# Channel products of an fp32-accurate token mixer: seven block products in place of eight

## The chip, the cores and the metric

One Trainium2 chip, one core of it. The metric is the device time of one execution in microseconds (us), the median of several runs. The engines are TensorE (PE, matmuls; PEld is its weight load), VectorE (DVE), ScalarE (ACT), GpSimd (POOL) and SyncE (SP, which issues the transfers).

## The reference, cut to what matters

An RWKV attention (8 heads of 48, 768 steps, batch 2) feeds a gated MLP with a token mix, and its result x (2, 768, 384) feeds the mixer that the change is about:

```python
def _moe2_ref(x, w_tok1, w_tok2, w_ch1, w_ch2) -> np.ndarray:
    xt = x.transpose(0, 2, 1)
    h = np.maximum(xt @ w_tok1, 0.0) @ w_tok2       # 768 -> 256 -> 768, over tokens
    u = x + h.transpose(0, 2, 1)
    h2 = np.maximum(u @ w_ch1, 0.0) @ w_ch2         # 384 -> 1536 -> 384, over channels
    return (u + h2).astype(np.float32)
```

The two products of the second line of h2 run over 2 x 768 = 1536 tokens. Everything is float32.

## The kernel before, in words

Each float32 operand is kept as two tiles, a rounded high part and the low rest, and `prod` (L254) makes one product as three matmuls into one PSUM tile: high times high (L257), high weight times low data (L258), low weight times high data (L259). The high part is written by ScalarE, the low part by a subtraction on VectorE or GpSimd. The weights arrive as 64-bit words and are converted in three stages (`advance`: two ScalarE instructions L214 and L215, two VectorE instructions L217 and L219, then ScalarE L224 for the high and GpSimd or VectorE L226 for the low part).

The program is written out by hand: `ORDER` and `LAST` are strings of letters, and each letter emits one piece of work, so they set in which order every engine meets its instructions. `LAST` covers the gated MLP's end, the conversions of the last weights (digits 0, 1, 2), the token products T1 (`i`, `j`) and T2 (`k`, `l`), and, as letter `m`, the first channel product C1 of the first token group. Then `rest` (L483) emits what is left in loops.

The channels are handled transposed: channels on the 128 partitions, tokens along the columns. Tokens stand in four groups of 384. `C1(h, j)` makes 128 of the 1536 hidden channels for group h: 3 blocks of input channels by 3 matmuls of 384 columns, then `relu_split` (L396) writes the high part `ch` on ScalarE (L398) and the low part `cl` on VectorE (L399). `C2(h, j, ct)` adds that hidden block into output block ct: 3 matmuls of 384 columns into a PSUM tile that stays for all 12 values of j. `rest` emits C1 for group h+1 and C2 for group h in turn, so that a hidden block is ready long before it is used. At j = 11 VectorE adds the residual (L454) and SyncE stores 128 x 384 values (L455).

Early in the program, `outputs` (L612) adds an already made tile `av` into the PSUM tile `py` with an identity matmul (L617) for the first seven 128-token blocks, between groups of sixteen or more 48-row matmuls (L608 before it, L623 behind it), and `kv` (L635) does the same for a 112 x 112 state tile.

## Time and profile before

| what | value |
|---|---|
| median of 3 runs (lowest, highest) | 391.27 us (390.36, 391.82) |
| the profiled execution: its time, its span | 391.98 us, 390.3 us |
| TensorE's granted clock | 1.00 in each stretch from 0 to 385 us |
| TensorE busy | 379.9 us, 97 % of the span |
| VectorE, ScalarE, GpSimd busy | 233.5, 187.8, 133.1 us |
| 254 to 385 us: TensorE, VectorE, GpSimd busy | 130.57, 36.93, 4.95 us of 131 |

The span is the profiled execution alone; its time has 1.7 us more around it. Busy time of an engine that is not the bound may grow without cost as long as nothing waits for it. The attention and the first parts of the gated MLP run to about 150 us, the gated MLP's token mix and output to about 213 us, T1, T2 and the first C1 tiles to about 254 us, and `rest` from there to the end.

### The profile page before, as it was taken

To read this page: it belongs to the slowest core of one execution; us is meant where nothing else is said; L and a number is where in the kernel's file an instruction comes from. 1 tells how busy PE (TensorE), PEld (TensorE's weight loads), DVE (VectorE), ACT (ScalarE), POOL (GpSimd) and SP (SyncE) were. 2 spreads that over 40 slices of the span, in tenths; PEclk is the share of its full clock that TensorE was granted. 3 is DMA by queue.
4 is the path that set the end of the run, shared out by engine and by line. 5 is a ranking of instruction groups with operands and counts; after the bars stand their busy time and mean duration, and the time that the engine had idled before them with its cause. 6 is when DMAs were issued, how large, how long until landed. Compare 5 with 4: busy or idle time off the path is not lost.

```text
span 390.3 us, 7950 instructions
## 1 busy us (share of the span) xinstructions
PE 379.9 (97%) x3229; PEld 354.8 (91%) x3229; DVE 233.5 (60%) x396; ACT 187.8 (48%) x427; POOL 133.1 (34%) x149
## 2 busy tenths in 40 slices
PE   8899999999999999999999999999999999999994
PEld 3487788889999799999999999999999999999993
DVE  7999998889797575794486674782133114211320
ACT  3699878887345795754546674741111111111000
POOL 2325577763543356567544651350000000000000
PEclk9999999999999999999999999999999999999998
DMA  7575375453361014322433242400010001000110
GB/s 238 172 215 181 100 246 155 122 156 114 94 214 42 2 40 123 107 66 71 123 102 102 81 126 78 121 3 0 3 44 18 1 0 62 0 2 0 64 40 27
DMA packets 15581, 33.68 MB, mean 86 GB/s; under 512 B 2352, under 2 KB 5680, under 8 KB 15536
## 3 DMA queue, kind: packets, MB, share of 16 engines
q1 hardware_dynamic: 15536, 33.09, 27.9%
q8 instruction: 27, 0.44, 0.5%
q14 instruction: 18, 0.15, 0.1%
HBM read 30.72 MB, written 2.36 MB: 85 GB/s over the span
## 4 chain that ended last, share of the span: by engine, by line
PE 83%; POOL 4%; ACT 3%; issue 3%; DVE 3%; DMA 2%; SPq 1%; POOLq 0%; ACTq 0%
PE mm L257 23%; PE mm L258 23%; PE mm L259 23%; PE py L623 3%; PE pa L582 2%; PE py L608 2%; DMA st<-in_dram 1%; PE tr L282 1%; POOL vs L367 1%; PE pkv L641 1%; DMA kr<-in_dram 1%; PE mm L567 1%; PE mm L420 1%; PE py L617 1%; PE pt L595 1%
## 5 line engine op out<-in xcount | busy, mean ns | idle before, releaser
L399 DVE SCALAR_TENSOR_TENSOR cl<-mm,ch 128x384 fp32r<-128x384 f32 x48 | 26.5, 556 | 83.9 <-ACT ch L398 83.9
L398 ACT ACTIVATE ch<-mm 128x384 fp32r<-128x384 f32 x48 | 23.4, 492 | 93.1 <-PE mm L259 93.0
L217 DVE SCALAR_TENSOR_TENSOR st<-st 128x384 int32<-128x384 int32 (+1 forms) x50 | 30.3, 607 | 9.5 <-ACT st L215 7.9
L219 DVE SCALAR_TENSOR_TENSOR st<-st 128x384 int32<-128x384 int32 (+1 forms) x50 | 33.2, 665 | 1.7
L214 ACT ACTIVATE st<-st 128x384 f32<-128x384 f32 (+1 forms) x50 | 25.8, 517 | 9.3 <-DMA st<-in_dram 9.3
L588 POOL TENSOR_SCALAR_AFFINE_SELECT A<-A 128x512 f32<-128x512 f32 x24 | 18.3, 770 | 33.5 <-ACT A L587 32.0
L215 ACT ACTIVATE st<-st 128x384 int32<-128x384 uint32 (+1 forms) x50 | 25.5, 510 | 0.0
L369 ACT ACTIVATE gh<-vs 128x384 fp32r<-128x384 f32 x16 | 8.4, 524 | 32.9 <-POOL vs L367 32.9
L367 POOL TENSOR_TENSOR vs<-vs,uT 128x384 f32<-128x384 f32 x16 | 19.2, 1205 | 11.6 <-DVE vs L365 11.6
L560 POOL TENSOR_TENSOR rk<-kr 112x512 f32<-112x512 f32 x12 | 19.0, 1580 | 11.4 <-DMA kr<-in_dram 11.4
L257 PE MATMUL mm<-xt,wuh 128*128 128x256 f32 x72 | 20.8, 289 | 0.0
L259 PE MATMUL mm<-xt,wul 128*128 128x256 f32 x72 | 20.3, 282 | 0.0
L258 PE MATMUL mm<-xt,wuh 128*128 128x256 f32 x72 | 20.3, 282 | 0.0
L534 DVE TENSOR_TENSOR_SCAN wf<-wf,scan 112x516 f32<-112x516 f32 x12 | 19.0, 1583 | 1.6 <-DMA wf<-in_dram 1.6
L548 DVE TENSOR_TENSOR_SCAN wf<-wf,scan 112x516 f32<-112x516 f32 x12 | 17.8, 1480 | 0.4
L391 POOL TENSOR_TENSOR x1l<-x,x1h 128x384 fp32r<-128x384 f32 x12 | 14.0, 1173 | 10.4 <-ACT x1h L390 10.4
L125 PE MATMUL mm<-scan 112*128 112x512 bf16 x49 | 14.2, 431 | 3.1 <-DVE scan L673 1.7
L556 DVE TENSOR_TENSOR kr<-kr,wf 112x1024 f32<-112x1024 f32 x12 | 15.9, 1328 | 1.2 <-DVE wf L548 0.2
L257 PE MATMUL mm<-ch,c20h 128*128 128x384 f32 x48 | 16.1, 336 | 0.2 <-DVE o L454 0.2
L257 PE MATMUL mm<-woh,gh 128*128 128x384 f32 x48 | 16.2, 338 | 0.0
L259 PE MATMUL mm<-woh,gl 128*128 128x384 f32 x48 | 16.1, 336 | 0.0
L257 PE MATMUL mm<-uh,c10h 128*128 128x384 f32 x48 | 16.1, 336 | 0.0
(188 smaller groups left out, 1233.3 us busy)
## 6 DMA issues: line engine op xcount, KB each, us to landing
st<-in_dram SPq DMA_DIRECT2D x38, 384.0 KB, 3.4
kr<-in_dram SPq DMA_DIRECT2D x12, 448.0 KB, 4.3
st<-in_dram SPq DMA_DIRECT2D x18, 256.0 KB, 4.2
wf<-in_dram SPq DMA_DIRECT2D x12, 227.5 KB, 2.9
vn<-in_dram SPq DMA_DIRECT2D x12, 192.0 KB, 4.5
out_dram<-o SPq DMA_DIRECT2D x12, 192.0 KB, 1.9
bsg<-in_dram SPq DMA_DIRECT2D x2, 192.0 KB, 3.9
ub<-in_dram SPq DMA_DIRECT2D x1, 3.5 KB, 4.6
```

The source lines that it names most:

```text
L214: nc.scalar.activation(high.bitcast(F32), high.bitcast(F32), AF.Copy, scale=REBIAS)
L215: nc.scalar.activation(low, low.bitcast(U32), AF.Copy, scale=TOP3, bias=FLOOR)
L217: nc.vector.scalar_tensor_tensor(low, high, -2 ** 31, low, op0=ALU.bitwise_and, op1=ALU.bitwise_or)
L219: nc.vector.scalar_tensor_tensor(low, high, 3, low, op0=ALU.logical_shift_left, op1=ALU.bitwise_or)
L257: mm(out, w[0], x[0], start=first, stop=False, skip_group_check=True)
L258: mm(out, w[0], x[1], start=False, stop=False, skip_group_check=True)
L259: mm(out, w[1], x[0], start=False, stop=last, skip_group_check=True)
L367: nc.gpsimd.tensor_tensor(t, t, self.uT[d, h], op=ALU.mult)
L398: nc.scalar.activation(hi, ps, AF.Relu)
L399: nc.vector.scalar_tensor_tensor(lo, ps, 0.0, hi.bitcast(F32), op0=ALU.max, op1=ALU.subtract)
L534: nc.vector.tensor_tensor_scan(WF[i][:, WCOL + 2:], WF[i][:, :NHP * CW], scan1.rearrange("p h c -> p (h c)"), 0.0, op0=ALU.mult, op1=ALU.add)
L560: nc.gpsimd.tensor_tensor(RK[i][:PR], KR[i][:, 0], KR[i][:, 1], op=ALU.mult)
```

## The change

**Blocks.** Tokens stand in three groups of 512 columns, split in two halves of 256 (`ONE`, `TWO`). The T2 tiles, which were four of 384, are 512, 256, 256 and 512 wide (`EDGES`). The hidden channels go in 6 steps of 256 for each group, 18 steps in all.

**Seven for eight.** With weights cut in 2 x 2 blocks of 128 x 128 and tokens in two halves, a product of 2 x 2 blocks takes eight block products; Strassen's scheme in Winograd's form takes seven, of sums of blocks. `C2` does so for output blocks 0 and 1 in all 18 steps (digits `1` to `7`); output block 2 stays plain (`C2d`, digits `8`, `9`). The first channel product does so for groups 1 and 2 (`C1s`, letters `g` to `m`, seven products of 256 columns and two plain ones of 512 for the third input block); group 0 stays plain, with 512 columns (`C1`, letters `a`, `b`).

**Sums.** The left sums are made once: of the second weights on GpSimd (`A`, `B`), of the first weights on VectorE with the low parts on GpSimd (`C`, `D`). The sums of u for groups 1 and 2 are made on VectorE (`E`, `F`). In each step the results of `C1s` are added from PSUM into SBUF on VectorE, made positive and rounded on ScalarE (`o`, `q`), and VectorE makes two low parts (`p`, `r`), four sums of halves (`s`) and two low parts of these sums (`t`, `u`).

**Banks.** Five PSUM banks hold the four sums and output block 2 for all six steps of a group; three rotate for the first channel product. At a group's end `G` to `P`, `Q`, `S` put the sums together and store eighteen pieces of 128 x 256. The residual (`R`) is added on GpSimd.

**Order.** A new string `REST` sets the order of all this. The letter `m` leaves `LAST` and the rest of `LAST` closes up, with the conversions of the channel weights at earlier places. The identity matmuls of the early stage are split in two: 64 and 64 output rows for `py`, 64 and 48 for the state.

```diff
+G = 2 * P
+ONE, TWO = slice(0, G), slice(G, 2 * G)
+EDGES = 0, 4, 6, 8, 12
...
+REST = (
+    "abAzAc deBacB fAb12d efBaC3 587695 7EbaFc D412d6 38Fe94 c1Ab2d fBa38c 579CRe AD64b1 Bad23f 89cebg 57612d fhAijC "
...
-    def C1(self, h, j):
-        ps = self.mm(E)
-        c = slice(j * P, (j + 1) * P)
-        for k in range(3):
-            self.prod(ps, self.wp(f"c1{k}", 0, c, DCH), self.u[h, k], k == 0, k == 2)
-        hi, lo = self.a2(F32R, E, "ch"), self.a15(F32R, "cl")
-        self.relu_split(ps, hi, lo)
-        self.hid[h, j] = hi, lo
-
-    def C2(self, h, j, ct):
-        n = DCH // P
-        if j == 0:
-            self.cps[ct] = self.mm(E, self.ps3)
-            hi, lo = self.u[h, ct]
-            self.o[ct] = self.a15(nm="o")
-            self.nc.vector.tensor_tensor(self.o[ct], hi.bitcast(F32), lo.bitcast(F32), op=ALU.add)
-        c = slice(ct * P, (ct + 1) * P)
-        self.prod(self.cps[ct], self.wp(f"c2{j // 4}", j % 4, c, E), self.hid[h, j], j == 0, j == n - 1)
-        if j == n - 1:
-            nc = self.nc
-            o = self.o[ct]
-            nc.vector.tensor_tensor(o, self.cps[ct], o, op=ALU.add)
-            nc.sync.dma_start(self.out[ct * P:(ct + 1) * P, h * E:(h + 1) * E], o)
...
+    def left_sums(self, e, f):
+
+        t = self.st("sw")
+        a11, a21, a12, a22 = (f[:, q * P:(q + 1) * P] for q in range(4))
+        s1, s2, s3, s4 = (t[:, q * P:(q + 1) * P] for q in range(4))
+        e(s1, a21, a22, op=ALU.add)
+        e(s2, s1, a11, op=ALU.subtract)
+        e(s3, a21, a11, op=ALU.subtract)
+        e(s4, a12, s2, op=ALU.subtract)
+        return t
...
+    def split_sums(self, e, t, to, place):
+
+        for (hi, lo), x in ((to, t[:, :3 * P]), (place, t[:, 3 * P:])):
+            self.nc.scalar.activation(hi, x, AF.Copy)
+
+    def sums_of_c2(self, k):
+
+        if k == 0:
+            self.sum_tiles("s2")
+        i, b = k // 2, k % 2 * 2
+        hi, lo = (t.rearrange("p (k c) -> p k c", c=E)[:, b:b + 2, :2 * P].bitcast(F32) for t in self.w[f"c2{i}"])
+        f = self.st("f")
+        e = self.nc.gpsimd.tensor_tensor
+        e(f.rearrange("p (k c) -> p k c", k=2), hi, lo, op=ALU.add)
+        self.sw["s2", k] = self.left_sums(e, f)
...
+        e = self.nc.vector.tensor_tensor
+        for q in range(2):
+            hi, lo = (t.bitcast(F32) for t in self.wp(f"c1{q}", 0, slice(k * G, (k + 1) * G), DCH))
+            e(f[:, q * G:(q + 1) * G], hi, lo, op=ALU.add)
+        self.sw["s1", k] = self.left_sums(e, f)
...
+        for q in range(2):
+            hi, lo = self.u[n + 1, q]
+            f.append(self.st("f"))
+            e(f[q], hi.bitcast(F32), lo.bitcast(F32), op=ALU.add)
+        ta, tb = self.ut = [self.st("ta"), self.st("tb")]
+        e(ta[:, ONE], f[0][:, TWO], f[0][:, ONE], op=ALU.subtract)
+        e(ta[:, TWO], f[0][:, TWO], f[1][:, TWO], op=ALU.subtract)
+        e(tb[:, ONE], f[1][:, TWO], ta[:, ONE], op=ALU.subtract)
+        e(tb[:, TWO], f[1][:, ONE], tb[:, ONE], op=ALU.subtract)
...
+    def C1(self, n, b):
+
+        p = self.mm(2 * G)
+        for q in range(3):
+            self.prod(p, self.C1w(n, b, q), self.u[0, q], q == 0, q == 2)
...
+    def sub(self, o, x, y):
+        self.nc.vector.scalar_tensor_tensor(o, x, 0.0, y, op0=ALU.max, op1=ALU.subtract)
+
+    def C1a(self, n):
+        r, ta, tb, p = self.raw[n][:4]
+        self.sub(ta[:, ONE], p[:, TWO], r[:, ONE])
+        h, l = self.hid[n][0]
+        self.sub(l, p, h.bitcast(F32))
+
+    def C1b(self, n):
+        r, ta, tb, p1, p2 = self.raw[n]
+        self.sub(ta[:, TWO], p1[:, TWO], r[:, TWO])
+        self.nc.vector.tensor_tensor(tb[:, ONE], r[:, TWO], ta[:, ONE], op=ALU.subtract)
+        self.sub(tb[:, TWO], p2[:, ONE], tb[:, ONE])
+        h, l = self.hid[n][1]
+        self.sub(l, p2, h.bitcast(F32))
+        self.raw[n] = [ta, tb]
...
+    def right_split(self, n, j):
+        t = self.raw[n][j]
+        hi, lo = self.big("th", "t"), self.big("tl", "t")
+        self.nc.scalar.activation(hi, t, AF.Copy)
+        self.nc.vector.tensor_tensor(lo, t, hi.bitcast(F32), op=ALU.subtract)
+        self.hid[n].append((hi, lo))
...
+    def C1s(self, n, m):
+
+        g, k = divmod(n, DCH // G)
+        w = lambda q: self.C1w(k, 1, 0) if q == 3 else [t[:, q * P:(q + 1) * P] for t in self.ws["s1"][k]]
+        half = lambda v, c: [t[:, c] for t in v]
+        b, c, d, ta, tb = (self.u[g, q] for q in range(5))
+        p, act = self.prod, self.nc.scalar.activation
+        add = lambda o, i, j: self.nc.vector.tensor_tensor(o, i, j, op=ALU.add)
+        if m == 0:
+            self.raw[n] = [self.mm(2 * G) for _ in range(3)] + [self.temp(q) for q in ("sz", "p1", "p2")]
+        x, y, z, sz, c1, c2 = self.raw[n]
+        if m == 0:
+            p(z[:, ONE], self.C1w(k, 0, 0), half(b, ONE), True, True)
+            p(z[:, TWO], w(0), half(ta, ONE), False, True)
+            act(sz, z, AF.Copy)
+        elif m == 1:
+            p(x, self.C1w(k, 0, 2), d, True, False)
+            p(x[:, ONE], self.C1w(k, 0, 1), half(c, ONE), False, True)
+        elif m == 2:
+            p(x[:, TWO], w(3), half(c, TWO), False, True)
+            add(c1, x, sz)
+        elif m == 3:
+            p(z[:, ONE], w(1), half(tb, ONE), False, True)
+            add(c1[:, TWO], z[:, ONE], c1[:, TWO])
+        elif m == 4:
+            p(y, self.C1w(k, 1, 2), d, True, False)
+        elif m == 5:
+            p(y[:, ONE], self.C1w(k, 1, 1), half(tb, TWO), False, True)
+            act(c2[:, ONE], y[:, ONE], AF.Copy)
+            add(c2[:, TWO], y[:, TWO], sz[:, TWO])
+        else:
+            p(z[:, ONE], w(2), half(ta, TWO), False, True)
+            two = lambda t: t.rearrange("p (a c) -> p a c", a=2)
+            add(two(c2), z[:, ONE].unsqueeze(1).to_broadcast([P, 2, G]), two(c2))
+            self.raw[n] = [c1, c2]
+            self.hid[n] = []
+
+    def C1r(self, n, j):
+        r, h, l = self.raw[n][j], self.big("h"), self.big("l")
+        self.nc.scalar.activation(r, r, AF.Relu)
+        self.nc.scalar.activation(h, r, AF.Copy)
+        self.hid[n].append((h, l))
+
+    def C1l(self, n, j):
+        h, l = self.hid[n][j]
+        self.nc.vector.tensor_tensor(l, self.raw[n][j], h.bitcast(F32), op=ALU.subtract)
+
+    def C1t(self, n):
+        c1, c2 = self.raw[n]
+        ta, tb = self.raw[n] = self.temp("ta"), self.temp("tb")
+        e = lambda o, i, j: self.nc.vector.tensor_tensor(o, i, j, op=ALU.subtract)
+        e(ta[:, ONE], c1[:, TWO], c1[:, ONE])
+        e(ta[:, TWO], c1[:, TWO], c2[:, TWO])
+        e(tb[:, ONE], c2[:, TWO], ta[:, ONE])
+        e(tb[:, TWO], c2[:, ONE], tb[:, ONE])
...
+    def C2(self, n, q):
+
+        g, k = divmod(n, DCH // G)
+        x = self.hid[n]
+        w = lambda q: self.C2w(k, 0, 1) if q == 3 else [t[:, q * P:(q + 1) * P] for t in self.ws["s2"][k]]
+        i, o, w, x, c = {
+            1: lambda: (0, ONE, self.C2w(k, 0, 0), x[0], ONE), 2: lambda: (2, ONE, self.C2w(k, 1, 0), x[1], ONE),
+            3: lambda: (2, TWO, w(3), x[1], TWO), 4: lambda: (3, ONE, self.C2w(k, 1, 1), x[3], TWO),
+            5: lambda: (1, ONE, w(0), x[2], ONE), 6: lambda: (0, TWO, w(1), x[3], ONE),
+            7: lambda: (1, TWO, w(2), x[2], TWO)}[q]()
+        self.prod(self.total(g, i)[:, o], w, [t[:, c] for t in x], k == 0 and q in (1, 2, 4, 5), k == DCH // G - 1)
+
+    def C2d(self, n, t):
+        g, k = divmod(n, DCH // G)
+        c = slice(t * G, (t + 1) * G)
+        for b in range(2):
+            self.prod(self.total(g, 4)[:, c], self.C2w(k, b, 2), [x[:, c] for x in self.hid[n][b]],
+                      k == 0 and t == 0 and b == 0, k == DCH // G - 1 and b == 1)
...
+        hi, lo = self.u[g, ct]
+        o = self.oo[:, 2 * ct * G:(2 * ct + 2) * G]
+        self.nc.gpsimd.tensor_tensor(o, hi.bitcast(F32), lo.bitcast(F32), op=ALU.add)
...
+    def finish(self, g, m):
+
+        nc, a, o = self.nc, {i: self.acc.get((g, i)) for i in range(4)}, self.o
+        s1, s2, s3, s4 = self.part
+        add = lambda to, x, y: nc.vector.tensor_tensor(to, x, y, op=ALU.add)
+        more = lambda to, x: nc.gpsimd.tensor_tensor(to, to, x, op=ALU.add)
+        if m == 0:
+            nc.scalar.activation(s1, a[0][:, ONE], AF.Copy)
+            more(o[0, 0], s1)
+        elif m == 1:
+            add(o[0, 0], a[2][:, ONE], o[0, 0])
+            self.store(g, 0, 0)
...
+    def finish_rest(self, g, t):
+        self.nc.vector.tensor_tensor(self.o[2, t], self.acc[g, 4][:, t * G:(t + 1) * G], self.o[2, t], op=ALU.add)
+        self.store(g, 2, t)
 
...
+        parts.update({q: later(self.C1s, m) for m, q in enumerate("ghijklm")})
+        parts.update({q: lambda i, t=t: self.finish_rest(i, t) for t, q in enumerate("QS")})
+        count = dict.fromkeys(parts, 0)
+        for part in REST.replace(" ", ""):
+            parts[part](count[part])
+            count[part] += 1
+
...
                 if i < ADDED:
-                    nc.tensor.matmul(PY[i], dn.ident, AV[i], start=(i % NC == 0), stop=False,
-                                     skip_group_check=True)
+                    for t in HALF:
+                        nc.tensor.matmul(PY[i][t], dn.ident[:, t], AV[i], start=(i % NC == 0), stop=False,
+                                         skip_group_check=True)
                 for h in range(H):
...
                 if i % NC and i < ADDED:
-                    nc.tensor.matmul(pkv, dn.ident[:PR, :PR], SC[1 - i % 2], start=False, stop=True,
-                                     skip_group_check=True)
+                    for q in (slice(0, 64), slice(64, PR)):
+                        nc.tensor.matmul(pkv[q], dn.ident[:PR, q], SC[1 - i % 2], start=False, stop=True,
+                                         skip_group_check=True)
                 KV[i] = pkv
...
+                i=dn.T1p, j=dn.T1e, k=dn.T2p, l=dn.T2e)
             parts = {key: turn(key, f) for key, f in parts.items()}
```

Line numbers of the changed kernel in the rows below: `prod`'s three matmuls are L270 to L272; L577 adds from PSUM in `C1s`, L615 is `C1l`, L620 `C1t`, L567 `right_split`.

**TensorE, inside `rest`.** Of before: the end of one C1 tile (mm_3720) and one step of C2 into the three standing tiles.

```order
L257 MATMUL mm_3720<-uh_3358,c12h_2911 128x384
L258 MATMUL mm_3720<-ul_3359,c12h_2911 128x384
L259 MATMUL mm_3720<-uh_3358,c12l_2912 128x384
L257 MATMUL mm_3538<-ch_3309,c22h_3484 128x384
L258 MATMUL mm_3538<-cl_3310,c22h_3484 128x384
L259 MATMUL mm_3538<-ch_3309,c22l_3485 128x384
L257 MATMUL mm_3544<-ch_3309,c22h_3484 128x384
```

Of the changed kernel, letters `h`, `i`, `j`, `k` of the fifth step that uses `C1s`; x is mm_4295, z mm_4297, y mm_4296, `uth` and `utl` a sum of u, `s1m` a sum of weights.

```order
L270 MATMUL mm_4295<-uh_3236,c11h_2276 128x256
L271 MATMUL mm_4295<-ul_3237,c11h_2276 128x256
L272 MATMUL mm_4295<-uh_3236,c11l_2277 128x256
L270 MATMUL mm_4295<-uh_3236,c10h_2163 128x256
L271 MATMUL mm_4295<-ul_3237,c10h_2163 128x256
L272 MATMUL mm_4295<-uh_3236,c10l_2164 128x256
L270 MATMUL mm_4297<-uth_3646,s1m_3528 128x256
L271 MATMUL mm_4297<-utl_3647,s1m_3528 128x256
L272 MATMUL mm_4297<-uth_3646,s1m_3528 128x256
L270 MATMUL mm_4296<-uh_3305,c12h_2823 128x512
L271 MATMUL mm_4296<-ul_3306,c12h_2823 128x512
L272 MATMUL mm_4296<-uh_3305,c12l_2824 128x512
```

Where one kind of matmul of 384 columns stood, there are now matmuls of 256 and of 512; z is written a second time here, after VectorE and ScalarE have read its first contents.

**VectorE, inside `rest`.** Of before: five C1 tiles, all that VectorE gets for them.

```order
L399 SCALAR_TENSOR_TENSOR cl_3567<-mm_3556,ch_3566 128x384
L399 SCALAR_TENSOR_TENSOR cl_3590<-mm_3579,ch_3589 128x384
L399 SCALAR_TENSOR_TENSOR cl_3613<-mm_3602,ch_3612 128x384
L399 SCALAR_TENSOR_TENSOR cl_3636<-mm_3625,ch_3635 128x384
L399 SCALAR_TENSOR_TENSOR cl_3659<-mm_3648,ch_3658 128x384
```

Of the changed kernel, one step's worth (p_697 and p_698 are the sums in SBUF of the fifth such step, p_674 and p_675 those of the step before it).

```order
L577 TENSOR_TENSOR p_697_4299<-mm_4295,sz_4298 128x512
L577 TENSOR_TENSOR p_697_4299<-mm_4297,p_697_4299 128x256
L577 TENSOR_TENSOR p_698_4300<-mm_4296,sz_4298 128x256
L615 TENSOR_TENSOR l_4331<-p_674_4167,h_4330 128x512
L615 TENSOR_TENSOR l_4386<-p_675_4168,h_4385 128x512
L620 TENSOR_TENSOR ta_4402<-p_674_4167 128x256
L620 TENSOR_TENSOR ta_4402<-p_674_4167,p_675_4168 128x256
L620 TENSOR_TENSOR tb_4403<-p_675_4168,ta_4402 128x256
L620 TENSOR_TENSOR tb_4403<-p_675_4168,tb_4403 128x256
L567 TENSOR_TENSOR tl_4409<-ta_4402,th_4408 128x512
L577 TENSOR_TENSOR p_698_4300<-mm_4297,p_698_4300 128x512
L567 TENSOR_TENSOR tl_4417<-tb_4403,th_4416 128x512
```

Six of 512 and six of 256 columns stand for what were two instructions of 384 for the same 256 channels; only the four L577 rows read PSUM, the eight others read SBUF alone. The new first step's results stand ahead of the step before's low parts.

**TensorE, in `LAST`, at T1 of the second batch.** Of before, one T1 product and a C1 tile of group 0 behind it; then of the changed kernel the same T1 product and what follows it.

```order
L259 MATMUL mm_3274<-x1h_3194,t1l_2514 128x384
L257 MATMUL mm_3299<-uh_2949,c10h_2205 128x384
L258 MATMUL mm_3299<-ul_2950,c10h_2205 128x384
L259 MATMUL mm_3299<-uh_2949,c10l_2206 128x384
```

```order
L272 MATMUL mm_3153<-x1h_3111,t1l_2503 128x384
L270 MATMUL mm_3172<-x1h_3015,t1h_2502 128x384
L271 MATMUL mm_3172<-x1l_3016,t1h_2502 128x384
L272 MATMUL mm_3172<-x1h_3015,t1l_2503 128x384
```

The twelve C1 tiles that filled such places are gone; the next T1 product follows at once.

## Rows read from the trace of the kernel before

**Rows 1.** The page, part 1: busy time and share of each engine.

```profile
PE 379.9 (97%) x3229; PEld 354.8 (91%) x3229; DVE 233.5 (60%) x396; ACT 187.8 (48%) x427; POOL 133.1 (34%) x149
```

**Rows 2.** Busy us by stretch: PE, PEld, DVE, ACT, POOL; clock, DMA share, GB/s.

```profile
213.00:254.00 41.00, 41.00 (x245) 40.79 (x244) 27.51 (x48) 25.57 (x58) 17.63 (x17) 1.00 0.33 97
254.00:385.00 131.00, 130.57 (x752) 129.68 (x750) 36.93 (x71) 20.51 (x43) 4.95 (x4) 1.00 0.05 18
```

**Rows 3.** What TensorE waited for: total us, times, longest.

```profile
PE mm L258 <- POOL t2l L226: 0.5, 1, 0.5
```

**Rows 4.** TensorE by line and form: busy us, mean ns, idle before.

```profile
L257 PE MATMUL mm<-ch,c20h 128*128 128x384 f32 x48 | 16.1, 336 | 0.2 <-DVE o L454 0.2
```

**Rows 5.** The timeline, TensorE: start, duration, instruction, at three widths.

```profile
62.06 0.28 PE L257 MATMUL mm<-xt,wuh 128*128 128x256 f32 x1
...
63.73 0.28 PE L259 MATMUL mm<-xt,wul 128*128 128x256 f32 x1
...
72.08 0.39 PE L258 MATMUL mm<-wvl,xt 128*128 128x512 f32 x1
...
73.69 0.39 PE L259 MATMUL mm<-wvh,xt 128*128 128x512 f32 x1
...
229.69 0.33 PE L259 MATMUL mm<-uh,c11l 128*128 128x384 f32 x1
...
235.06 0.33 PE L257 MATMUL mm<-uh,c10h 128*128 128x384 f32 x1
```

**Rows 6.** The timeline, VectorE: instructions of three widths.

```profile
64.73 0.67 DVE L325 TENSOR_TENSOR vl<-v,vh 128x512 fp32r<-128x512 f32 x1
65.33 0.55 DVE L217 SCALAR_TENSOR_TENSOR st<-st 128x384 int32<-128x384 int32 x1
...
171.93 0.43 DVE L219 SCALAR_TENSOR_TENSOR st<-st 128x256 int32<-128x256 int32 x1
172.27 0.55 DVE L388 TENSOR_TENSOR x<-mm,x 128x384 f32<-128x384 f32 x1
```

**Rows 7.** The timeline, VectorE and GpSimd, 244 to 249 us.

```profile
244.06 0.55 DVE L217 SCALAR_TENSOR_TENSOR st<-st 128x384 int32<-128x384 int32 x1
244.65 0.56 DVE L219 SCALAR_TENSOR_TENSOR st<-st 128x384 int32<-128x384 int32 x1
245.13 0.55 DVE L430 TENSOR_TENSOR ul<-mm,uh 128x384 fp32r<-128x384 f32 x1
245.46 2.33 POOL L226 TENSOR_TENSOR c21l<-st,c21h 128x384 fp32r<-128x384 f32 x2 [10.30 <-ACT c21h L224]
245.59 1.31 DVE L217 SCALAR_TENSOR_TENSOR st<-st 128x384 int32<-128x384 int32 x1
246.94 1.27 DVE L219 SCALAR_TENSOR_TENSOR st<-st 128x384 int32<-128x384 int32 x1
248.14 1.01 DVE L430 TENSOR_TENSOR ul<-mm,uh 128x384 fp32r<-128x384 f32 x2
```

**Rows 8.** The timeline, GpSimd: additions and subtractions of three widths.

```profile
81.82 1.29 POOL L560 TENSOR_TENSOR rk<-kr 112x512 f32<-112x512 f32 x1
...
173.28 0.75 POOL L226 TENSOR_TENSOR t1l<-st,t1h 128x256 fp32r<-128x256 f32 x1 [2.61 <-ACT t1h L224]
...
190.61 1.03 POOL L226 TENSOR_TENSOR t2l<-st,t2h 128x384 fp32r<-128x384 f32 x1 [1.07 <-ACT t2h L224]
```

**Rows 9.** ScalarE and VectorE by line: busy us, mean ns, idle before.

```profile
L398 ACT ACTIVATE ch<-mm 128x384 fp32r<-128x384 f32 x48 | 23.4, 492 | 93.1 <-PE mm L259 93.0
...
L399 DVE SCALAR_TENSOR_TENSOR cl<-mm,ch 128x384 fp32r<-128x384 f32 x48 | 26.5, 556 | 83.9 <-ACT ch L398 83.9
```

**Rows 10.** The chain that ended last, in the early stage: start, us.

```profile
26.18 0.65 PE py L617 x2
...
30.22 0.81 PE py L608 x16
31.03 0.84 PE py L617 x2
```

152 lines of the change are left out of this document (116 added, 36 removed), and 4 rows, old and new, of the table REST.

## The prediction

> **What bounds the kernel now.** I read the page first: TensorE is busy 97 % of the span, VectorE 60 %, ScalarE 48 %, GpSimd 34 % [rows 1]. An average over stages says little, so the table by stretches comes next [rows 2]. In the stretch that the change rewrites, 254 to 385 us, TensorE works 130.57 of 131 us at full granted clock while VectorE has 36.93 us of work and GpSimd 4.95. TensorE's waits confirm it: from T2 on it waited once for GpSimd, 0.5 us [rows 3], and once, 0.2 us, for an output tile [rows 4]. So a microsecond of TensorE work taken out of this stretch is a microsecond of time, as long as no other engine takes TensorE's place. The other engines have room there: VectorE idles 84 us ahead of its `cl` subtractions and ScalarE 93 us ahead of `ch` [rows 9].
>
> **What the change takes from TensorE.** Back-to-back starts on the timeline give what a matmul costs, since the printed durations overlap [rows 5]: 256 columns (63.73 - 62.06) / 14 = 0.1193 us, 512 columns (73.69 - 72.08) / 7 = 0.230 us, 384 columns (235.06 - 229.69) / 31 = 0.1732 us. The channel products are 18 groups of 48 matmuls of 384 before (one group is [rows 4]), so 864 x 0.1732 = 149.6 us. In the changed order I count 846 of 256 and 180 of 512: 100.9 + 41.4 = 142.3 us. Seven for eight is not an eighth: the third blocks and group 0's first product stay plain, so columns fall from 331,776 to 308,736 (7 %), and a column of a 256-wide matmul costs 0.466 ns, of a 384-wide one 0.451. T2 goes from 72 x 0.1732 = 12.47 to 36 x 0.230 + 36 x 0.1193 = 12.57. Together **-7.2 us**.
>
> **What it gives VectorE.** Prices from starts [rows 6]: 512 columns 65.33 - 64.73 = 0.60 us, 256 columns 172.27 - 171.93 = 0.34, 384 about 0.47; for 128 I estimate 0.21 along the same line. An instruction that needs the result of the one before it costs 0.12 more (244.06 to 244.65 is 0.59 against 0.47) [rows 7]. A step that uses `C1s` now holds six instructions of 512 and six of 256 columns, where two of 384 stood. GpSimd, nearly empty here before, gets the sums of the second weights, low parts and residuals, at 1.29, 1.03 and 0.75 us for 512, 384 and 256 columns [rows 8] and an estimated 0.48 for 128. ScalarE gets 3,840 columns a step, at 492 ns per 384 [rows 9] 4.9 us of a step of 21 x 0.1193 + 6 x 0.230 + 33 x 0.1193 = 7.8 us, and stays hidden.
>
> I add these prices up along the new order, stretch by stretch. The tight one runs from the second part of the first `C1s` step (`h`) to the last product of the fifth (`m`): TensorE 35.9 us; VectorE 26 x 0.60 + 43 x 0.34 + 16 x 0.21 + 12 x 0.12 = 35.0 us, because the last left sums of the first weights and the sums of u for group 2 fall into it too; GpSimd 3 x 1.29 + 5 x 1.03 + 3 x 0.75 + 9 x 0.48 = 15.6 us. Elsewhere there is room: from the first plain step to the first `C1s` 39.1 of TensorE against 27.6 of VectorE and 28.5 of GpSimd, from the fifth `C1s` step's end to the end 54.7 against 47.1 and 11.5.
>
> **VectorE beside GpSimd.** The trace shows a price for running both on SBUF [rows 7]: two VectorE instructions took 1.07 us alone (244.06 to 245.13), and the same two 2.55 us (245.59 to 248.14) while GpSimd ran two subtractions, 2.33 us. VectorE lost 1.48 us in 2.33, that is 0.64 of GpSimd's time. In the tight stretch 0.66 of VectorE's time is in instructions whose two inputs are both SBUF, like those two; the others read PSUM, like the subtractions of u, of which two went through in 1.01 us [rows 7]. I take the loss as 0.64 x 0.66 = 0.42 of GpSimd's time, 6.6 us. Then VectorE needs 41.6 us where TensorE has 35.9, and is 5.7 late. What is late next: the row that adds product `j` from bank z, and behind it on VectorE the low parts and sums that `t` and `u` hand to the second products; TensorE stops at `m`, which writes z again. Between `j` and `m` of that step TensorE has 3.9 us of other products, less some 0.5 for the read itself: 3.4 us are absorbed. Stall: 5.7 - 3.4 = **+2.3 us**. Bounds: no loss, no stall; the whole of GpSimd's time lost, 35.0 + 15.6 - 35.9 - 3.4 = 11.3. I take the middle value since it is measured on the same pair of engines.
>
> The Trainium skill ("SBUF — State Buffer", section "Who interferes with whom") says that a VectorE instruction with two SBUF inputs and a GpSimd instruction that reads SBUF exclude each other, and that whoever starts first holds the pair for its whole length. The trace agrees in kind (0.55 us became 1.31 and 1.27) but shows 0.64 of GpSimd's time lost, not all of it. By the rule the stall would be 6.0 us in place of 2.3; that case stands below as a rival.
>
> **The start of `rest`.** Between 213 and 254 us VectorE works 27.51 of 41 us [rows 2]. The twelve C1 tiles that leave this place take 108 x 0.1732 = 18.7 us of TensorE with them, but only 12 x 0.556 = 6.7 of VectorE [rows 9]: 20.8 us remain in 22.3, and conversions have moved to earlier places. What filled TensorE's gaps between dependent T1 and T2 products is gone. The trace has no such stretch; from below nothing, from above two more hits like that in [rows 7], 3.0 us. I take the size of the one wait there is now [rows 3] and a little: **+0.7**.
>
> **The end.** After the last `m` TensorE has 11.1 us of products; the chain on VectorE (last low parts, sums, low parts, final additions) is 9.2 us, and GpSimd works 6.4 beside it: 9.2 + 0.42 x 6.4 = 11.9. I take **+0.6** (0 to 2). The last addition has 256 columns in place of 384, 0.34 against 0.47: -0.1. Eighteen stores for twelve lie beside the products, except the last, as now.
>
> **The early identity matmuls.** One takes 0.84 us on the chain, full width; the sixteen 48-row products before it, 96 columns each, 0.81 [rows 10], which is 0.53 ns a column against 1.09 (two passes of 384 columns in 0.84). So two halves of 64 rows should run side by side and cost what one does: 0. If they did not, each half would cost what the whole does at its shortest, 7 x 0.65 = +4.6; if all of what the longest has above the shortest goes, 7 x 0.19 = -1.3.
>
> **Sum:** -7.2 + 2.3 + 0.7 + 0.6 - 0.1 = -3.7, from the profiled execution's 391.98 us to 388.3. That execution is 0.7 above the median of 391.27, which makes 387.6; I say 387.5.
>
> **The rivals.**
> - No stall: VectorE stays ahead. For it: 35.0 against 35.9 us without a loss. Against: the loss in [rows 7]. 391.27 - 7.2 = 384.0, or 382.7 with the 1.3 of the identity matmuls. Chance 0.20 (382.5 to 385).
> - My sum, with a loss of 0.3 to 0.55 of GpSimd's time: 385 to 389.3. Chance 0.42.
> - VectorE behind GpSimd becomes the bound, and the loss is all of GpSimd's time under two-input instructions: 0.66 x 15.6 = 10.3, stall 35.0 + 10.3 - 35.9 - 3.4 = 6.0; 391.27 - 7.2 + 6.0 + 1.2 = 391.3 (392.7 if the end pays by the same measure). For it: 1.31 and 1.27 us for an instruction of 0.55 [rows 7]. Against: 0.64. 389.3 to 393.2, chance 0.23.
> - Slower: VectorE loses GpSimd's time whatever it reads. The stall is 15.6 f - 4.3 for a lost share f, and it outweighs the other terms by 2 us from f = 0.79 on. At f = 1 it is 11.3, so 391.27 - 7.2 + 11.3 + 1.2 = 396.6. Against it: the two reads of PSUM at 1.01 us. Chance 0.15.
>
> A measurement of this kernel can tell about 0.5 %, 2 us, from no change: the bounds are 389.3 and 393.2. Faster 0.62 (the first two), same 0.22, slower 0.16. The likeliest case's own range is 385 to 389.3; the range for 8 in 10 goes from 382.5 (no stall) to 393.0 (the third case).
>
> **What the changed profile would show.** Channel products at the three pitches above, with TensorE's busy time about 7 us lower. One or two waits of TensorE for VectorE at the second write of z, 1 to 3 us together, in the fourth or fifth `C1s` step, and VectorE near 90 % busy for 30 us before them, its two-input rows at up to 1.3 us where GpSimd's low parts run. T1 and T2 close up, with less than 1 us of waits. The early identity matmuls take the same 0.6 to 0.85 us in twice the pieces. ScalarE stays well below TensorE. Wrong would make it: VectorE's 256-column rows at more than 0.34 us (43 of them in the tight stretch, so 0.05 more is 2 us); ScalarE's added round trips holding z or the hidden blocks; or a granted clock below 1.00 behind a stall, which no stretch of [rows 2] shows.

## The result, and the profile after

The changed kernel takes 386.59 us, median of 4 runs (386.32 to 387.11), against 391.45 us (390.36 to 391.82, with one run more than the 391.27 above): the ratio is 0.9882 with a 95 % interval from 0.9859 to 0.9905. It is 1.2 % faster; 387.5 was forecast, in a range from 382.5 to 393.0. The profiled execution took 386.76 us, its span 384.7.

The page of the changed kernel, busy time by engine, answers to [rows 1]:

```profile
PE 372.4 (97%) x3413; PEld 336.6 (87%) x3413; DVE 330.8 (86%) x598; ACT 245.3 (64%) x542; POOL 197.5 (51%) x221
```

TensorE is still busy 97 %, but VectorE went from 60 to 86 %. Where, the table by stretches says (columns as in [rows 2]): from the first channel product to the first seven-for-eight step of the first product, through the stretch that the prediction called tight, on to the last channel product, and the end.

```profile
230.72:272.44 41.72, 41.48 (x253) 36.84 (x251) 36.48 (x70) 23.02 (x55) 36.01 (x48) 1.00 0.00 1
272.44:308.84 36.40, 36.12 (x275) 34.24 (x274) 33.66 (x82) 21.08 (x44) 12.56 (x15) 1.00 0.06 19
308.84:377.96 69.12, 66.35 (x505) 62.30 (x504) 64.04 (x130) 37.41 (x69) 14.95 (x13) 1.00 0.06 21
377.96:384.70 6.74, 0.15 (x2) 0.00 (x0) 0.42 (x1) 0.00 (x0) 0.00 (x0) 0.75 0.21 68
```

VectorE (third pair) works 33.66 of 36.40 us and then 64.04 of 69.12, where it had 36.93 of 131 before [rows 2]. TensorE's waits, total, times and longest, answer to [rows 3, 4]:

```profile
PE mm L271 <- DVE tl L567: 1.6, 2, 1.4
PE mm L270 <- DVE o L702: 0.6, 1, 0.6
...
PE mm L270 <- DVE o L672: 0.3, 1, 0.3
PE mm L270 <- DVE p L577: 0.3, 1, 0.3
PE mm L270 <- DVE fi L1022: 0.2, 1, 0.2
```

All are waits for VectorE. The view names whole waits only; many small ones lie below it, so I go by starts: the pitch of a matmul is the time from its start to the next one's. The first channel product, two stretches of undisturbed ones, and the last (TensorE's timeline, as in [rows 5]):

```profile
230.72 0.40 PE L270 MATMUL mm<-uh,c10h 128*128 128x512 f32 x1
...
240.26 0.39 PE L270 MATMUL mm<-uh,c10h 128*128 128x512 f32 x1
...
242.07 0.39 PE L272 MATMUL mm<-uh,c12l 128*128 128x512 f32 x1
...
249.91 0.28 PE L270 MATMUL mm<-th,c20h 128*128 128x256 f32 x1
...
253.33 0.28 PE L272 MATMUL mm<-th,c20l 128*128 128x256 f32 x1
...
377.84 0.28 PE L272 MATMUL mm<-h,c22l 128*128 128x256 f32 x1
```

Eight starts apart, 512 columns cost 0.226 us; 29 apart, 256 columns cost 0.118. The medians over all 1,026 products are 0.227 and 0.117. At these, the products are 846 x 0.117 + 180 x 0.227 = 139.8 us; the first starts at 230.72 and the last ends, one pitch after its start, at 377.96: 147.2 us. So 7.4 us are waits. (One median for all 256-wide matmuls is a little rough: the 252 that read u or its sums have a pitch of 0.119 to 0.120, those from the hidden tiles 0.116 to 0.117, so that about 0.5 of the 7.4 us is pitch.)

**Where the 5.6 us of span went**, summed from starts in the two traces:

| piece | before | after | difference | forecast |
|---|---|---|---|---|
| channel products, undisturbed | 149.6 | 139.8 | -9.8 | -7.3 |
| waits among them, the flag's matmul with them | 0.7 | 7.4 | +6.7 | +3.6 |
| T2 products and the waits behind each | 14.4 | 13.6 | -0.8 | +0.1 |
| transposes that T2 and its input need | 4.3 | 3.2 | -1.1 | 0 |
| identity matmuls of the early stage and the products behind them | | | -0.6 | 0 |
| one wait at 14 us | 1.4 | 0.4 | -1.0 | 0 |
| last product's end to the span's end | 5.7 | 6.8 | +1.1 | -0.1 |

The flag is a check that the program makes once: VectorE compares sums from the early stage with limits, one small matmul adds up the outcomes, and the program branches on the result. Several runs below move that matmul. The wait at 14 us is no work of the change (see the end); the profiled execution of before had its longer form, which fits its 391.98 us, above every one of the four runs.

### The profile page after: what moved, and what is told of

Its sections match the earlier page's. It is cut to its first block, busy times and chain, and to the rows that moved or that the text cites. A ratio compares the mean times of both kernels' runs of the same rounds, so it can differ in the third digit from the quotient of the medians.

```text
span 384.7 us, 8799 instructions
## 1 busy us (share of the span) xinstructions
PE 372.4 (97%) x3413; PEld 336.6 (87%) x3413; DVE 330.8 (86%) x598; ACT 245.3 (64%) x542; POOL 197.5 (51%) x221
## 4 chain that ended last, share of the span: by engine, by line
PE 68%; DVE 19%; ACT 6%; issue 3%; DMA 2%; SPq 1%; POOL 0%; DVEq 0%; ACTq 0%
PE mm L270 19%; PE mm L271 19%; PE mm L272 19%; DVE p L577 4%; DVE tl L567 3%; DVE l L615 2%; PE py L883 2%; PE pa L841 2%; DVE tb L620 2%; DVE ta L620 2%; DMA st<-in_dram 2%; PE py L867 1%; PE mm L826 1%; PE mm L434 1%; PE tr L295 1%
## 5 line engine op out<-in xcount | busy, mean ns | idle before, releaser
L232 DVE SCALAR_TENSOR_TENSOR st<-st 128x384 int32<-128x384 int32 (+1 forms) x50 | 35.3, 706 | 1.7
L230 DVE SCALAR_TENSOR_TENSOR st<-st 128x384 int32<-128x384 int32 (+1 forms) x50 | 32.9, 657 | 2.4 <-ACT st L228 2.4
L673 POOL TENSOR_TENSOR o<-o,part 128x256 f32<-128x256 f32 x9 | 7.4, 834 | 42.0 <-ACT part L675 29.6
L819 POOL TENSOR_TENSOR rk<-kr 112x512 f32<-112x512 f32 x12 | 20.3, 1689 | 11.5 <-DMA kr<-in_dram 11.5
L663 POOL TENSOR_TENSOR o<-uh,ul 128x512 f32<-128x512 f32 x9 | 14.6, 1650 | 19.7 <-DMA out_dram<-o 12.3
L566 ACT ACTIVATE th<-ta 128x512 fp32r<-128x512 f32 x18 | 11.4, 632 | 15.4 <-DVE ta L620 13.3
L270 PE MATMUL mm<-xt,wuh 128*128 128x256 f32 x72 | 20.8, 289 | 0.0
L272 PE MATMUL mm<-xt,wul 128*128 128x256 f32 x72 | 20.3, 282 | 0.0
L610 ACT ACTIVATE h<-p 128x512 fp32r<-128x512 f32 x24 | 15.2, 633 | 7.5 <-PE mm L271 5.2
L793 DVE TENSOR_TENSOR_SCAN wf<-wf,scan 112x516 f32<-112x516 f32 x12 | 18.0, 1499 | 1.7 <-DMA wf<-in_dram 1.7
L807 DVE TENSOR_TENSOR_SCAN wf<-wf,scan 112x516 f32<-112x516 f32 x12 | 16.7, 1396 | 0.4
L609 ACT ACTIVATE p<-p 128x512 f32<-128x512 f32 x24 | 14.9, 621 | 2.5 <-DVE p L577 2.3
L577 DVE TENSOR_TENSOR p<-mm,sz 128x512 f32<-128x512 f32 (+1 forms) x24 | 13.2, 550 | 3.6 <-ACT p L598 3.2
L615 DVE TENSOR_TENSOR l<-p,h 128x512 fp32r<-128x512 f32 x24 | 16.2, 682 | 0.0
L270 PE MATMUL mm<-woh,gh 128*128 128x384 f32 x48 | 16.2, 337 | 0.0
```

Source lines behind the costliest of these rows:

```text
L230: nc.vector.scalar_tensor_tensor(low, high, -2 ** 31, low, op0=ALU.bitwise_and, op1=ALU.bitwise_or)
L232: nc.vector.scalar_tensor_tensor(low, high, 3, low, op0=ALU.logical_shift_left, op1=ALU.bitwise_or)
L270: mm(out, w[0], x[0], start=first, stop=False, skip_group_check=True)
L272: mm(out, w[1], x[0], start=False, stop=last, skip_group_check=True)
L577: add = lambda o, i, j: self.nc.vector.tensor_tensor(o, i, j, op=ALU.add)
L615: self.nc.vector.tensor_tensor(l, self.raw[n][j], h.bitcast(F32), op=ALU.subtract)
```

## Experiments

Twelve kernels answer three questions: what the seven products bring, what makes the 7.4 us of waits, and what the end costs. "Waits" below is always the time from the first to the last channel product less the products at their median pitch in that run.

**Neither product by seven for eight: both plain, 512 columns.**

```diff
-            self.prod(p, self.C1w(n, b, q), self.u[0, q], q == 0, q == 2)
+            self.prod(p, self.C1w(n % 6, b, q), self.u[n // 6, q], q == 0, q == 2)
...
+        self.prod(self.total(g, ct), self.C2w(k, b, ct), self.hid[n][b], k == 0 and b == 0, k == DCH // G - 1 and b == 1)
...
-        parts.update({q: later(self.C1s, m) for m, q in enumerate("ghijklm")})
```

> Both channel products plain, in the groups of 512 columns, no sums of blocks at all; every other stage as in the changed kernel. Theory (the seven-for-eight products give back in stalls what they save): products 648 x 0.2273 = 147.3 us, where the changed kernel has 139.9 us of products and 7.3 us of waits from its first channel product to its last; VectorE has little to do, so waits stay under 1 us: 385.5 to 387.5 us, the same as the changed kernel within 0.5 %. Rival (the gain comes from seven for eight): the wider columns alone bring 149.5 - 147.3 = 2.2 us against the kernel before: 389 to 390 us, slower than the changed kernel by more than 0.5 %.

Measured: 393.33 us, ratio 1.0052 (1.0031 to 1.0074). 3.3 us of it are one wait: I had put the flag's matmul too early in the loop (the longest wait of TensorE in this run is for VectorE's `okc`, 3.0 us). So once more with the flag later:

> As the run with both channel products plain in columns of 512, but the matmul of the flag stands five products later, so that TensorE no longer waits 3.3 us there for a flag that VectorE has not made yet. 2.8 us less than that run's 393.3: 390.5 (389.8 to 391.2), within 0.5 % of the kernel before: the wider groups of tokens alone bring nothing, since a column costs 0.455 ns in a matmul of 512 from the hidden tiles as it does in one of 384. Rival (the loop's order has other waits): 392 us or more.

Measured: 388.50 us, ratio 0.9943 (0.9926 to 0.9959). Neither expectation held. From first to last product this run takes 149.98 us, as before (150.3): wider columns bring nothing there, because a product of 512 columns from the hidden tiles costs more than one from `u`. TensorE's timeline of this run, first three products of `h`, then of `uh`:

```profile
300.25 0.39 PE L268 MATMUL mm<-h,c20h 128*128 128x512 f32 x1
...
301.65 0.39 PE L268 MATMUL mm<-uh,c10h 128*128 128x512 f32 x1
...
303.71 0.39 PE L268 MATMUL mm<-h,c21h 128*128 128x512 f32 x1
```

Six from `h` take 1.40 us, 0.233 each; nine from `uh` 2.06, 0.229 (0.227 in their median). And yet the kernel is 2.3 us faster than before. What it shares with the changed kernel is all that lies ahead of the products: T1 and T2 closed up, the wider T2 tiles, the early matmuls. So of the change's 4.8 us, 2.3 come without any seven-for-eight, and some 2.5 (0.9943 to 0.9882) from it; the two intervals together leave about 1 us either way.

**Only the second product by seven for eight**, the first plain, in an order that I wrote as a loop.

> First channel product plain in all three groups, second by seven for eight in all; a simple order written as a loop. Theory (VectorE's lateness comes from the sums of the first product, which add four instructions on VectorE and a round trip to each step): products 18 x (18 x 0.2273 + 33 x 0.1171) = 143.2 us and 1 to 3 us of waits, most at the ends of the groups: 383.5 to 385.5 us. Rival (the second product's sums and the ends of the groups make the waits): 5 us or more of waits remain, 387 us or more.

Measured: 390.61 us, ratio 0.9992 (0.9974 to 1.0010). The time is the rival's, but not by its waits: there are 4.6 us of them, of which 1.7 are for the first low parts on GpSimd and 1.0 at the last step, and 9.5 us pass from the last product to the end, where the changed kernel has 6.8. Both come from the loop's order and stand near the first and the last of these products, at 239 and 375 us. Between 272.4 and 308.8 us, where every step has its second product by seven, the waits are 0.3 us. As a time the run is inconclusive; for the step itself it speaks for the theory.

**Only the first product by seven for eight**, in the changed kernel's order with the letters left out that fall away.

```diff
+        for ct, b in {1: ((0, 0), (1, 0)), 2: ((0, 1),), 3: ((1, 1),)}[q]:
+            self.prod(self.total(g, ct), self.C2w(k, b, ct), self.hid[n][b], k == 0 and b == 0, k == DCH // G - 1 and b == 1)
```

> First channel product by seven for eight in groups 1 and 2, second plain in all, in the changed kernel's order with the letters left out that are not needed. Theory: products 24.5 + 45.9 + 73.6 = 144.1 us; VectorE loses four sums and two low parts a step, GpSimd the sums of the second weights, so under 1.5 us of waits: 383.5 to 385.5 us. Rival (the round trip of the first product through bank z makes the waits, whatever VectorE's load): 3 us or more of waits in the steps of groups 1 and 2, 386.5 us or more.

Measured: 386.58 us, ratio 0.9882 (0.9863 to 0.9902), the changed kernel's time to 0.01 us. The time is the rival's, its reason is not: the waits fell to 1.5 us, as the theory wants it, and the products took 147.1, not 144.1, since the plain second product pays the 0.233 of the hidden tiles. The round trip through bank z is in this kernel too, and makes no 3 us of waits: that rival fell. Its stretches (as above) show what the waits went with:

```profile
272.00:309.00 37.00, 36.92 (x231) 32.80 (x230) 22.83 (x54) 15.38 (x32) 4.49 (x6) 1.00 0.07 22
309.00:371.00 62.00, 62.00 (x391) 55.71 (x391) 36.22 (x60) 26.29 (x51) 10.94 (x8) 1.00 0.04 14
```

VectorE has 22.83 and 36.22 us here, against 33.66 of 36.40 and 64.04 of 69.12: at 60 % load TensorE doesn't wait, at 92 % it does. Behind 309 us VectorE's instructions lost 3.3 us to GpSimd in this run too, by their lengths over the undisturbed ones, and TensorE still didn't wait for them.

**Is it GpSimd beside VectorE?** The longest wait of the changed kernel looks like it. Its timeline at 321 us:

```profile
320.85 0.42 DVE L620 TENSOR_TENSOR tb<-p,ta 128x256 f32<-128x256 f32 x1
321.22 4.47 POOL L663 TENSOR_TENSOR o<-uh,ul 128x512 f32<-128x512 f32 x3 [12.26 <-DMA out_dram<-o]
321.30 1.52 DVE L620 TENSOR_TENSOR tb<-p,tb 128x256 f32<-128x256 f32 x1
...
322.74 1.78 DVE L567 TENSOR_TENSOR tl<-ta,th 128x512 fp32r<-128x512 f32 x1
...
324.58 0.39 PE L271 MATMUL mm<-tl,s2m 128*128 128x256 f32 x1 [1.35 <-DVE tl L567]
```

When group 0's stores have landed, GpSimd starts three residual additions; `tb` begins 0.08 us later and takes 1.52 us, where the same form took 0.42 just before; `tl` takes 1.78 where it takes 0.68 alone, and the product that needs `tl` comes 1.5 us late. Three experiments on it. First, move these additions ahead, one at a time (the letters `R` in `REST`; the lines below show the tiles that this needs):

```diff
-        o = self.oo[:, 2 * ct * G:(2 * ct + 2) * G]
+        o = self.oo[:, 2 * ct * G:(2 * ct + 2) * G] if g else self.a2(nm="o")
```

> The changed kernel with the three residual additions of group 1 on GpSimd moved: they run one by one among the steps before, not three in a row when group 0's stores have landed (group 0's output tiles stand in free tiles of u's pool). Theory (two-input VectorE instructions stand still while GpSimd runs beside them): the wait of 1.5 us before product 5 of the fifth seven-for-eight step and the 0.5 us behind it go, and single additions are absorbed: 1.5 to 2.0 us faster than the changed kernel, 384.6 to 385.1. Rival (VectorE is full there anyway, and the same loss comes back at another place): within 0.5 us of the changed kernel, 386.1 to 387.1.

Measured: 387.92 us, ratio 0.9919 (0.9895 to 0.9943). The wait at 324 us is gone, and the waits are 8.4 us: 1.6 now stand at 293.6 us, and 0.5, 0.7 and 0.9 between 307 and 317. The time is above both ranges, and the rows show why:

```profile
290.75 1.31 POOL L662 TENSOR_TENSOR o<-uh,ul 128x512 f32<-128x512 f32 x1
290.78 1.83 DVE L567 TENSOR_TENSOR tl<-ta,th 128x512 fp32r<-128x512 f32 x1
```

Each moved addition met an instruction of VectorE with two SBUF inputs again: `tl` here lost 1.15 us, and `l` 1.07 and 1.05 us at 301.83 and 311.29. So this run moves the collision and can't tell it from a VectorE that is full. Second, the six additions of groups 1 and 2 on VectorE itself:

```diff
-        self.nc.gpsimd.tensor_tensor(o, hi.bitcast(F32), lo.bitcast(F32), op=ALU.add)
+        e = self.nc.vector if g else self.nc.gpsimd
+        e.tensor_tensor(o, hi.bitcast(F32), lo.bitcast(F32), op=ALU.add)
```

> The changed kernel with the six residual additions of groups 1 and 2 on VectorE in place of GpSimd (the first of group 1 a few letters later, behind the stores that it waits for). Theory (a GpSimd addition on SBUF keeps two-input VectorE instructions standing for about its own length): VectorE pays 0.6 us for each addition itself and no longer some 0.7 to 1.1 us of standing still: within 0.7 us of the changed kernel, 385.9 to 387.3. Rival (GpSimd's additions run beside VectorE and cost it nothing): 6 x 0.6 = 3.6 us more on an engine that is full there: 2.5 to 3.6 us slower, 389 us or more.

Measured: 387.62 us, ratio 0.9925 (0.9906 to 0.9945), 8.2 us of waits: between the two, 1.0 above the changed kernel in place of 0 or 2.5, and 2.1 us of its waits are one at the very end, where the last additions now stand in VectorE's queue. Third, without them:

```diff
+        if g:
+            self.nc.scalar.activation(o, hi.bitcast(F32), AF.Copy)
```

> The changed kernel with the residual of groups 1 and 2 copied by ScalarE from the high parts alone; the additions of the low parts are left out, so the output lacks them. Nothing is added to VectorE or GpSimd, and 6 x 1.29 = 7.7 us go from GpSimd. Theory (the additions made VectorE stand still): the waits before product 5 of the fifth seven-for-eight step and just behind go (1.5 + 0.3 + 0.2): 1.5 to 2.5 us faster than the changed kernel, 384.1 to 385.1. Rival (VectorE is behind there by its own work): within 0.5 us of it, 386.1 to 387.1.

Measured: 386.32 us, ratio 0.9881 (0.9861 to 0.9901), 6.6 us of waits. From 309 us on no instruction of VectorE is lengthened any more, where 3.5 us were lost before. The wait at 324 us is gone here too, but only 0.8 us of waits in all: others came, of 0.6 and 0.7 us at 332.7 and 373.8. The rival held. So the event at 321 us is real, but what it delays is late anyway a little further on.

**Is it VectorE's own work?** The same kernel, banks, order and round trips, with 14.4 us taken from VectorE:

```diff
-        self.nc.vector.tensor_tensor(l, self.raw[n][j], h.bitcast(F32), op=ALU.subtract)
+        self.nc.scalar.activation(l, h.bitcast(F32), AF.Copy)
```

> The changed kernel with the low parts of the hidden blocks of groups 1 and 2 written by ScalarE as copies of the high parts, in place of VectorE's subtractions: this leaves the subtraction out, so that the output is not the reference's, and takes 24 instructions of 512 columns (14.4 us) from VectorE and puts 24 x 0.63 us on ScalarE. Everything else, banks, order and round trips too, stays. Theory (VectorE's own work in the steps with both seven-for-eight products makes the waits, and GpSimd beside it only moves them): the 7.4 us of waits between first and last channel product fall to 3 us or less: 381.5 to 383.0 us. Rival (the round trip through bank z, ScalarE and back makes them): 6 us or more stay, 385.5 us or more.

Measured: 381.55 us, ratio 0.9742 (0.9722 to 0.9762), 2.65 us of waits. Its stretches:

```profile
272.00:309.00 37.00, 36.98 (x285) 35.35 (x285) 31.98 (x81) 25.16 (x52) 13.16 (x16) 1.00 0.06 19
309.00:371.00 62.00, 61.99 (x489) 59.77 (x487) 50.38 (x105) 45.64 (x85) 12.12 (x10) 1.00 0.05 16
```

TensorE works 61.99 of 62 us; VectorE 50.38. GpSimd has what it had, and ScalarE 45.64 us without harm. Even the collision of 321 us is still there:

```profile
318.72 1.32 POOL L663 TENSOR_TENSOR o<-uh,ul 128x512 f32<-128x512 f32 x1 [10.62 <-DMA out_dram<-o]
...
318.79 1.53 DVE L620 TENSOR_TENSOR tb<-p,tb 128x256 f32<-128x256 f32 x1
320.25 1.80 DVE L567 TENSOR_TENSOR tl<-ta,th 128x512 fp32r<-128x512 f32 x1
```

The same two instructions lose the same 2.2 us, and TensorE doesn't wait behind them. So 5.0 us of the changed kernel's time hang on these 24 instructions of VectorE, in the steps that use both products by seven for eight. What the run doesn't separate is their length from their place in VectorE's order: on ScalarE they take no turn there at all.

**A version from that: each group with one of the two.** The second product by seven in group 0 (where the first is plain), the first in groups 1 and 2.

> Each group has seven products for eight in one of its two channel products only: the second product in group 0, as in the changed kernel, the first in groups 1 and 2, whose second product is plain (as in the run with the second product plain everywhere). Theory (a step with both leaves VectorE no time, a step with either leaves enough): from the first to the last channel product 24.6 + 23.2 + 45.9 + 50.4 = 144.1 us of products and under 2 us of waits, and a shorter end (1.2 us): 383.0 to 385.0 us, faster than the changed kernel. Rival (the waits belong to the round trip of the first product): 3 us or more of waits in groups 1 and 2, 386 us or more.

Measured: 385.25 us, ratio 0.9864 (0.9844 to 0.9883), 0.25 above the theory's range, with waits of 1.9 us as it wants them. In this kernel the fourth left sum of the second weights overwrites a block that groups 1 and 2 need, so its output isn't the reference's. With that sum in a tile of its own, for which the ring of the sums' tiles had to go from 8 to 5, and the flag later:

> Each group has seven products for eight in one of its channel products only, as in the run before of that name, with the fourth left sum of the second weights in a tile of its own (the plain second product of groups 1 and 2 needs the block that it overwrote), and with the flag and the read of block 2's bank placed as in the run on the end. 0.4 us each less than that run's 385.25: 384.0 to 385.0 us, 1.6 % faster than the kernel before and faster than the changed kernel. Rival (the smaller ring of the sums' tiles makes group 0 wait): 386 us or more.

Measured: 389.78 us, ratio 0.9952 (0.9934 to 0.9969). The flag again: moved one product later, its sum came later in VectorE's queue as well, and TensorE stopped 2.4 us for it. The table by stretches shows the clock there:

```profile
240.00:246.00 6.00, 5.22 (x20) 4.34 (x21) 3.53 (x10) 1.98 (x6) 5.84 (x9) 0.72 0.00 0
246.00:260.00 14.00, 14.00 (x93) 12.78 (x93) 10.48 (x24) 6.41 (x15) 5.56 (x7) 1.00 0.01 2
```

0.72 over 6 us is a part of them at half the clock (the last section has the stretch). So with the flag's sum in its old place and only its matmul later:

> Seven products for eight in only one channel product of each group: the second in group 0, the first in groups 1 and 2 (the version that gave 385.25 us with one block of the second weights overwritten), here with the fourth left sum in a tile of its own. The flag's sum is made where the changed kernel makes it, but its matmul stands one product later, so that TensorE does not stop for it; the first half of block 2 is read after the last product of its bank. Theory (VectorE's work in a step with both is what makes the waits): as that run, 0.4 us less for the flag and 0.4 for the bank: 384.0 to 385.0 us, and the ratio to the kernel before 0.983 to 0.986, better than the changed kernel's. Rival (the smaller ring of the sums' tiles makes group 0 wait, or the flag's wait comes back as in the two runs that moved it): 386 us or more.

Measured: 387.21 us, ratio 0.9902 (0.9882 to 0.9922). The flag no longer stops TensorE, but the rival held: group 0's last sums wait for the smaller ring, and the run falls 1.5 us behind the one above between 268 and 293 us. ScalarE's row there is the first below. The second is SyncE's, at the end: the fourth of six stores took 2.25 us to issue, and the end is 1.3 us longer.

```profile
276.67 0.63 ACT L565 ACTIVATE th<-ta 128x512 fp32r<-128x512 f32 x1 [4.05 <-PE mm L271]
...
377.43 2.25 SPq L674 DMA_DIRECT2D out_dram<-o  x1
```

**The end.** The changed kernel's last rows show 6.1 us from VectorE's last result to the end of the span, where before there were 4.9 (385.33 to 390.28):

```profile
378.11 1.42 SPq L666 DMA_DIRECT2D out_dram<-o  x1
378.15 0.42 DVE L702 TENSOR_TENSOR o<-mm,o 128x256 f32<-128x256 f32 x1 [0.74 <-PE mm L272]
379.62 0.39 SPq L666 DMA_DIRECT2D out_dram<-o  x1
```

The last store is ready at 378.57, but SyncE is in the issue of the fifth store, 1.42 us where the others take 0.33, and issues the last at 379.62. Fewer stores, then:

```diff
-            self.store(g, 0, 1)
+            self.store(g, 0, None)
```

> The changed kernel with three small edits outside the steps: at a group's end blocks 0 and 1 are stored as one 128 x 512 piece each in place of two (four stores in the last 5 us in place of six); the flag's matmul stands one product later; the first half of output block 2 is read after the last product of its bank, not between two of them. Theory: the fifth store's issue takes 1.2 to 1.5 us on SyncE since four others are under way, and that delays the last; with four stores in all it is gone: -1.0; the flag -0.4 and the bank -0.4 as far as the waits of 0.52 and 0.77 us show: 384.3 to 385.3 us, and 5.1 us or less from VectorE's last instruction to the end of the span, where the changed kernel has 6.1. Rival (the end is the last store's own landing, and waits taken at one place come back at the next): 0.5 us or less, 386.0 to 387.0.

Measured: 388.89 us, ratio 0.9953 (0.9928 to 0.9977). (In groups 0 and 1 the merged store of block 1 goes out ahead of the last addition to it, so the output lacks that.) No issue took over 0.55 us any more, but the end still lasts 6.15 us: the last store landed 3.6 us after its issue, where it took 2.4. The flag cost 2.35 us here too. The wait before the last product of block 2 went. The time is above both ranges; without the flag's 2.35 it would be 386.5, inside the rival's. Nothing gained.

## Why the prediction was right, and where not

**The sum.** Forecast for the channel products with their waits -3.7 us, measured -3.1; for the whole -3.7, measured -4.86 between medians. That it fits so well is luck: a saving that was too small, waits that were too short and a start with the wrong sign cancel.

**TensorE's saving** was under-priced: -9.8 where -7.3 stood. The row for 256 columns [rows 5] came from products with `xt` at 62 us, 0.1193; the median here is 0.117, and 846 x 0.0023 is 1.9 us (or 1.4, when only the 594 from the hidden tiles are counted). 512 columns gave 0.227 in place of 0.230, 0.5 us.

**The step that failed is "VectorE beside GpSimd".** It took a loss of 0.64 from one collision [rows 7], spread it evenly over the tight stretch, 6.6 us, and got one stall of 2.3 us at `m`. In that stretch VectorE's instructions ran at their undisturbed lengths but for one, 0.12 us longer; TensorE waited 1.2 us, of which 0.13 stand at the fifth `m` (308.84 us), where 2.3 were forecast; no other `m` waits over 0.11. GpSimd's 12.56 us lay beside instructions that read PSUM, or waited themselves:

```profile
273.64 0.68 DVE L567 TENSOR_TENSOR tl<-tb,th 128x512 fp32r<-128x512 f32 x1
273.73 1.77 POOL L663 TENSOR_TENSOR o<-uh,ul 128x512 f32<-128x512 f32 x1
274.25 0.68 DVE L577 TENSOR_TENSOR p<-mm,sz 128x512 f32<-128x512 f32 x1
```

Here `tl`, with two SBUF inputs, came first and kept its 0.68 us; GpSimd's addition took 1.77 us, where 1.29 is the undisturbed length [rows 8], and ran on beside `p`, which reads PSUM. The Trainium skill ("SBUF — State Buffer", section "Who interferes with whom") says that issue order decides who blocks. The rows at 321 us agree: GpSimd came 0.08 us first, and VectorE lost 1.1 us. So a share of GpSimd's time was the wrong term: what counts is which instruction of VectorE stands beside each of GpSimd's, and which of the two came first.

**The waits lie behind it.** Of the 7.4 us, 5.5 fall after 308.84 us, where I had found room (54.7 against 47.1) and priced only 0.6 at the end. Four instructions of VectorE lost 3.5 us to GpSimd there, by their length over the undisturbed one; but without the additions behind these only 0.8 us of waits went, and without 14.4 us of VectorE's own work 4.7. A load of 86 % by my sum is no room when each result is needed within a step: VectorE still idles 5.1 us of that stretch (69.12 less 64.04), 2.5 of it in two waits for ScalarE, and what it is late by then isn't caught up. Nor is load alone the measure: from 230.72 to 272.44, in steps with only the second product by seven, VectorE was 87 % busy and lost some 6 us to GpSimd, and TensorE waited 0.7. I had priced load, not lateness. This last point is argued from the rows; no run changes the order alone.

**The start** was wrong in sign: T1 and T2 closed up without new waits and gained 1.9 us, +0.7 stood in the sum. I had read one wait there [rows 3], but that view leaves out the small ones: by starts T2's products took 14.4 us in the kernel before, where 72 undisturbed ones take 12.5, so there were waits to be saved. That this gain is the change's own, apart from the products, the plain kernel shows (0.9943). Which of its edits ahead of the products makes it wasn't tried.

**The end** cost 1.1 us more, not 0.1 less. The last store is issued 1.05 us after VectorE's last result, where it was 0.03 before; it then lands 0.5 us sooner (2.4 us for 3.0), and 0.7 us more pass behind its landing, which no run explains.

**The early identity matmuls** cost nothing, as forecast. [rows 10] has 0.84 and 0.65 for one; the two halves of one lie side by side. Before, then after:

```profile
26.02 0.81 PE L617 MATMUL py<-av,ident 128*128 128x384 f32 x2
26.75 1.14 PE L623 MATMUL py<-vn,A 128*64 128x48 f32 x32
```

```profile
25.16 0.87 PE L877 MATMUL py<-av,ident 128*64 128x384 f32 x4
25.86 1.09 PE L883 MATMUL py<-vn,A 128*64 128x48 f32 x32
```

Four instructions are 0.70 us from start to start, where two were 0.73 (26.02 to 26.75).

**The rivals.** No stall fell, with 7.4 us of waits. VectorE as the bound came true in part: the waits are VectorE's, but most of them come from its own instructions, and they took 6.7 of 9.8 us, not all. That VectorE loses GpSimd's whole time fell: it lost 0.12 us in the stretch on which that case rested.

## What to carry to other kernels

A scheme that saves matmuls by sums of blocks pays in vector instructions: count these per step, not per kernel, and price the lateness of the last result, not only the load. Here one of the two products by seven for eight gave as much as both (386.58 and 386.59 us). Before a wait is taken for a collision, take the colliding work out instead of moving it: moved, it collided again here; taken out, 3.5 us of collisions were worth 0.8 us of waits.
